# Fused attention and feed-forward kernel: fold of w3 and w_out moved into batch 0's attention, group 0's products behind it

## Chip, cores and metric

One core of a Trainium2 chip. The metric is the device time of one execution in microseconds. The kernel before takes 327.4 us (median of three runs, 326.2 to 327.7). An execution more than 1.5% above the fastest of its kernel counts as slow.

## The reference, cut to what matters

```python
# q, k, v: 8 batches x 8 heads x 576 x 64, f32
scores = q @ k.T / sqrt(64), masked to 0 <= i - j < 64      # causal window
attn   = softmax(scores) @ v                                 # -> x: 4608 x 512
a = x @ w1;  b = x @ w2                                      # 512 x 1024 each
out = ((a * b) @ w3) @ w_out                                 # 1024 x 1024, 1024 x 512
```

Nothing nonlinear lies between w3 and w_out, so the kernel forms their product once (the **fold**, 1024 x 512) and multiplies a*b by it.

## The kernel before: the parts concerned

PE does the matmuls; ACT, DVE and GpSimd (POOL in profiles) copy, mask and multiply; SP issues loads. PE writes into PSUM buffers, and a buffer can be used again when another engine has read it. PE is called warm when its granted clock is 1.0 (a matmul of 512 columns every 0.216 us in these traces) and cold at half of it (every 0.427 us).

Work goes in batches (attention, six steps each) and in groups of 512 tokens (eight blocks of a*b, four output blocks). The instructions of an engine stand in the order of the program, and one that waits holds up those behind it: in the change ACT stands idle for 5.21 us in front of a cast while copies that PE needs stand behind it. Line numbers in profiles are those of the kernel that was run; the same statement has other numbers in other versions.

```python
ps_s, ps_v, ps_t: one buffer each;  ps_f: bufs=3      # PSUM: scores, values, transposes, the rest

def scores(d):      # PE: 4 matmuls -> s_ps;  ACT: exp -> pt;  GpSimd: two masks a part
def values(d):      # PE: 8 matmuls -> o_ps;  ACT: ln, ln, exp;  DVE: two multiplies -> xT
def ffn_ab(g, fc):  # PE: 8 matmuls -> a_ps, b_ps (ps_f);  ACT: copy of a;  DVE: times b -> ab
def ffn_o(g, t):    # PE: 8 matmuls ab x wc -> ps_f;  DVE: copy;  store
def fold_t(fc):     # PE: 8 transposes of w3 -> ps_f;  DVE: copy
def fold_mm(fc):    # PE: 8 matmuls with w_out -> ps_f;  ACT: cast -> wc
...
load_qk(0, "k"); load_qk(0, "q")               # on the SP queue
...
pool_cp(gate, raws["k", 0][0:1, 0, 0:1])       # start gate: GpSimd waits for a first piece of k
for c in (0, 2, 3): load_v(0, c)               # all v and weight loads are on GpSimd's queue
for i in range(2): load_w12(i)
for c in (4, 5): load_v(0, c)
ones_of(1)                                     # memset for batch 1's v, on GpSimd
load_wo()
...  # batch 0: scores and values, with pieces of group 0's a*b between them (cut)
...  # then loads of w3, fold steps 0 to 2, batch 1's transposes, fold step 3
scores(6); fold_step(4); scores(7); values(6); fold_step(5); scores(8); values(7)
...  # and so on: one fold step, later one output block, beside each step of batch 1
```

From group 1 on, a schedule places a*b and output blocks between the attention steps; the change does not touch its principle.

## Time and profile before

| | before |
|---|---|
| last fold product on PE, started | 84.5 us |
| first a*b of group 1, started | 98.3 us |
| useful PE time lost until then | 45.9 us |
| the same, until 180 us | 53.6 us |
| time | 327.4 us |

The slices of the granted clock show that in this kernel PE is mostly warm after the opening. (The opening and later gaps hold dummy matmuls, `keep_busy`, whose results nobody reads; they are meant to keep the clock up.) Each digit is one of 40 equal slices, in tenths:

```profile
PEclk9765979998999789999999999999999999999796
```

### The profile page before, as it was taken

The page shows a single profiled execution, that of the slowest core. Times are in us where ns is not written, and L with a number is a line of the kernel's source. Part 1 is how long each engine was busy: PE and PEld are TensorE (multiplying, and loading weights), DVE is VectorE, ACT ScalarE, POOL GpSimd, SP SyncE. Part 2 cuts the span into 40 slices and gives each one's busy share as a digit, 9 for nine tenths or more (in the row PEclk, how much of TensorE's full clock was granted, in tenths as well). Part 3 has the DMA queues.
Part 4 walks back from the last instruction along what each step waited for, and adds up shares of the span by engine and source line. Part 5 has one row for each costly group of instructions (what it writes and reads, how often), then busy time and mean ns, then how long its engine had stood idle before and what let it go on. Part 6 is the DMA issues. An engine that isn't in the chain of part 4 may idle for free.

```text
span 327.4 us, 5810 instructions
## 1 busy us (share of the span) xinstructions
PE 285.9 (87%) x2151; PEld 177.9 (54%) x2151; DVE 195.6 (60%) x299; ACT 185.2 (57%) x308; POOL 178.6 (55%) x214
## 2 busy tenths in 40 slices
PE   4477599958899699999999999999999999996880
PEld 4465498535454455655555589555555555442330
DVE  5842545462378457977777776669767656545240
ACT  2246644656845367678778766487678766532200
POOL 8736493006891789679777856496785552200000
PEclk9765979998999789999999999999999999999796
DMA  7999969500049969496587664680293030030021
GB/s 214 314 341 250 198 106 180 59 0 0 3 82 253 306 157 89 161 246 42 119 297 65 94 214 144 70 134 3 22 162 21 2 123 7 2 130 2 4 98 41
DMA packets 52247, 38.91 MB, mean 119 GB/s; under 512 B 39360, under 2 KB 42432, under 8 KB 52208
## 3 DMA queue, kind: packets, MB, share of 16 engines
q0 software_dynamic: 41808, 9.96, 32.6%
q1 hardware_dynamic: 10400, 28.47, 24.5%
q8 instruction: 19, 0.31, 0.4%
q14 instruction: 20, 0.16, 0.2%
HBM read 38.80 MB, written 9.44 MB: 147 GB/s over the span
## 4 chain that ended last, share of the span: by engine, by line
PE 72%; DMA 11%; ACT 5%; DVE 4%; issue 3%; POOL 2%; SPq 0%; DVEq 0%; POOLq 0%; ACTq 0%
PE f_ps L392 36%; PE f_ps L405 18%; DMA w_sb<-in_moe_w_dram 8%; PE o_ps L306 6%; PE s_ps L271 4%; PE f_ps L451 4%; DMA stage<-in_k_dram 4%; PE tp L248 3%; ACT ln_s L316 1%; ACT r L318 1%; DVE xT L322 1%; POOL v L230 1%; DVE qT L257 1%; POOL k L215 1%; PE f_ps L443 1%
## 5 line engine op out<-in xcount | busy, mean ns | idle before, releaser
L392 PE MATMUL f_ps<-xT,w_sb 128*128 128x512 f16 (+3 forms) x768 | 139.9, 334 | 4.0 <-DVE xT L322 2.9
L392 PEld LDWEIGHTS <-w_sb 128*128 128x128 f16 x768 | 70.3, 100 | 51.3 <-issue 7.7
L285 POOL TENSOR_SCALAR_AFFINE_SELECT pt<-pt 128x512 f16<-128x512 f16 (+1 forms) x64 | 52.7, 823 | 82.4 <-ACT pt L276 82.4
L405 PE MATMUL f_ps<-wc_sb,ab 128*128 128x512 f16 x288 | 67.1, 379 | 0.1
L398 DVE TENSOR_TENSOR ab<-f_ps,a_sb 128x512 f16<-128x512 f32 (+1 forms) x74 | 49.9, 676 | 27.0 <-PE f_ps L392 25.1
L321 DVE TENSOR_TENSOR xT<-o_ps,r 64x384 f16<-64x384 f32 x48 | 26.4, 550 | 59.1 <-ACT r L318 59.1
L276 ACT ACTIVATE pt<-s_ps 128x1024 f16<-128x1024 f32 (+1 forms) x48 | 45.7, 952 | 27.5 <-PE s_ps L271 26.0
L397 ACT COPY a_sb<-f_ps 128x512 f32<-128x512 f32 (+1 forms) x74 | 42.0, 567 | 32.7 <-PE f_ps L392 32.1
L287 POOL TENSOR_SCALAR_AFFINE_SELECT pt<-pt 128x512 f16<-128x512 f16 (+1 forms) x64 | 52.7, 823 | 4.4
L315 ACT ACTIVATE ln_s<-o_ps 64x384 f32<-64x384 f32 x48 | 23.4, 487 | 36.8 <-PE o_ps L306 36.7
L405 PEld LDWEIGHTS <-ab 128*128 128x128 f16 x288 | 27.0, 98 | 27.6 <-issue 0.3
L230 POOL DMA_DIRECT2D v<-in_v_dram x40 | 34.1, 858 | 3.9 <-DMA v<-in_v_dram 2.1
L306 PE MATMUL o_ps<-pt,v 128*128 128x128 f16 (+1 forms) x384 | 29.0, 220 | 6.2 <-DVE xT L322 2.2
L306 PEld LDWEIGHTS <-v 128*128 128x128 f16 x384 | 24.8, 101 | 16.1 <-issue 2.7
L271 PE MATMUL s_ps<-qT,kT 128*128 128x256 f16 x192 | 28.7, 275 | 4.0 <-DVE qT L257 3.1
L407 DVE COPY t2k<-f_ps 128x512 f32<-128x512 f32 x36 | 24.9, 691 | 8.8 <-PE f_ps L405 8.0
L322 DVE TENSOR_TENSOR xT<-o_ps,r 64x384 f16<-64x384 f32 x48 | 26.9, 561 | 0.6
L271 PEld LDWEIGHTS <-kT 128*128 128x128 f16 x192 | 18.8, 103 | 15.0 <-issue 5.5
L318 ACT ACTIVATE r<-ln_s 128x384 f32<-128x384 f32 x48 | 25.1, 522 | 1.5
L316 ACT ACTIVATE ln_s<-o_ps 64x384 f32<-64x384 f32 x48 | 23.2, 482 | 0.6
L257 DVE COPY qT<-tp 64x768 f16<-64x768 f16 x18 | 17.3, 961 | 7.9 <-ACT qT L257 7.6
L252 DVE COPY kT<-tp 128x768 f16<-128x768 f16 x18 | 17.1, 950 | 3.9 <-PE tp L248 3.8
(52 smaller groups left out, 208.0 us busy)
## 6 DMA issues: line engine op xcount, KB each, us to landing
stage<-in_k_dram SPq DMA_DIRECT2D x32, 288.0 KB, 4.0
stage<-in_q_dram SPq DMA_DIRECT2D x32, 288.0 KB, 5.5
out_dram<-t2k SPq DMA_DIRECT2D x36, 256.0 KB, 2.0
v<-in_v_dram POOLq DMA_DIRECT2D x32, 128.0 KB, 4.0
w_sb<-in_moe_w_dram POOLq DMA_DIRECT2D x4, 512.0 KB, 24.1
ab<-in_moe_w_out_dram POOLq DMA_DIRECT2D x1, 1024.0 KB, 24.3
ab<-in_moe_w_dram POOLq DMA_DIRECT2D x4, 256.0 KB, 5.1
xT<-in_moe_w_dram POOLq DMA_DIRECT2D x4, 256.0 KB, 9.5
```

The lines of the kernel that those rows point to most:

```text
L230: nc.gpsimd.dma_start(out=vh[lo:P, c], in_=v[b, :, s0:s0 + P - lo, :].rearrange("h s d -> s h d"))
L271: nc.tensor.matmul(s_ps[:, jj, c0:c0 + 2 * n].rearrange("k (a n) -> k a n", a=2), kT[:, 2 * jp + jj, k0:k0 + P], qT[:, 2 * jp + jj, :, q0: ...
L276: nc.scalar.activation(pt[:, :, 0:w], s_ps[:, :, 0:w], AF.Exp, bias=-SHIFT, scale=scale)
L285: nc.gpsimd.affine_select(out=sl, in_=sl, pattern=pat, compare_op=ALU.is_ge, fill=0.0, base=off, channel_multiplier=-1)
L287: nc.gpsimd.affine_select(out=sl, in_=sl, pattern=[[-s, m] for s, m in pat], compare_op=ALU.is_ge, fill=0.0, base=63 - off, channel_multip ...
L306: nc.tensor.matmul(o_ps[:, jj, o0:o0 + n], v16[:, si * 2 + bi, j0 + jj, a * D:a * D + P], pt[:, jj, c0 + a * n:c0 + a * n + n], start=firs ...
L318: nc.scalar.activation(r, y, AF.Exp, scale=-1.0)
L322: nc.vector.tensor_tensor(xs[D:P], o_ps[D:P, :, 192:384], r[D:P], ALU.mult)
L392: nc.tensor.matmul(d[:, f * n + c0:f * n + c1], w[:, dc, (fc + f) * P:(fc + f + 1) * P], xT[:, dc, xc:xc + c1 - c0], start=first, stop=(dc ...
L397: act_cp(a_sb[:, 0:nf * n], a_ps[:, 0:nf * n])
L398: nc.vector.tensor_tensor(ab[:, fc:fc + nf, lo:hi], b_ps[:, 0:nf * n].rearrange("p (f n) -> p f n", f=nf), a_sb[:, 0:nf * n].rearrange("p ...
L405: nc.tensor.matmul(o_ps, ab[:, fc, t * P:t * P + P], wc_sb[:, fc, :], start=(fc == 0), stop=(fc == 7))
```

## The change

Intent: use the time in which PE waits for w1 and w2. w_out and w3 are loaded first, the fold goes between batch 0's steps; w1 and w2 come last, as all of group 0's a*b follows the fold; its output goes between batch 1's steps. Loads of batch 1's k and q, which ran beside the weights, are held back by a one-column memset into their buffer, which DVE does only after fold step 6; those of batch 2 by one on GpSimd.

The diff, cut to its core:

```diff
-    def load_qk(b, which):
+    def load_qk(b, which, gate=None):
         t = sb.tile([P, 2, TI * D], FP32, name="stage", bufs=4)
+        if gate is not None:
+            gate(t[:, 0, 0:1], 0.0)
...
     make_identity(nc, ident16)
+    load_wo()
+    load_w3(0)
+    load_w3(1)
...
-    pool_cp(gate, raws["k", 0][0:1, 0, 0:1])
     for c in (0, 2, 3):
         load_v(0, c)
-    for i in range(2):
-        load_w12(i)
+    load_w3(2)
     for c in (4, 5):
         load_v(0, c)
+    load_w3(3)
+    for half in range(2):
+        for i in range(2):
+            load_w12(i, half)
     ones_of(1)
-    load_wo()
...
+    for d in range(6):
+        if d < 5:
+            scores(d + 1)
+        if d == 3:
+            copy_v(0, 4)
+        if d < 5:
+            fold_step(d + 1)
+        values(d)
+    fold_step(6)
+    load_qk(1, "k", nc.vector.memset)
+    load_qk(1, "q")
+    fold_step(7)
...
+    for c in range(3):
+        cast_third(1, "k", c, act_cp if c != 1 else dve_cp)
+    for c in range(3):
+        cast_third(1, "q", c, act_cp if c != 1 else pool_cp)
+    for c in (0, 2, 3, 4, 5):
+        load_v(1, c)
+    for fc in range(8):
+        ffn_ab(0, fc)
+        if fc in (4, 5, 6):
+            transposes(1, "k", fc - 4)
...  # q transposes of batch 1
+    ffn_o(0, 0)
+    scores(6)
+    load_qk(2, "k", nc.gpsimd.memset)
...
+    for d in range(6, 12):
+        values(d)
+        if d < 10:
+            scores(d + 2)
+        if d in (7, 9):
+            ffn_o(0, (d - 3) // 2)
...
-        first = 3 if g == 1 else 0
+        first = 5 if g == 1 else 0
```

Batch 2's q transposes move to the fourth, fifth and sixth a*b block of group 1.

More of the change, by code (lines that the diff above doesn't have):

```diff
@@ L239, with transposes @@
     kTs = {}
-    def transposes(b, which, c, early=False):
+    def transposes(b, which, c, tp=None, late=True):
         if c == 0 and which == "k":
@@ L245, in transposes @@
         t16 = (k16s if which == "k" else q16s)[b]
-        tp = ps_f.tile([P, 6, P], FP16, name="f_ps") if early else ps_t.tile([P, 6, P], FP16, name="tp")
+        if tp is None:
+            tp = ps_t.tile([P, 6, P], FP16, name="tp")
         for i in range(6):
@@ L250, in transposes @@
         if which == "k":
-            cp = act_cp if early and c == 1 else dve_cp
+            cp = dve_cp if late or c != 1 else act_cp
             cp(kTs[b].rearrange("q j (p i) -> q j p i", i=TI)[:, :, :, 6 * c:6 * c + 6], src)
@@ L422, in w3_rows, with load_w12 @@
             xT[:, fc - 4, 2 * S:2 * S + DF].rearrange("p (a n) -> p a n", a=2)
-    def load_w12(i):
-        for half in range(2):
-            cols = slice(half * 512, half * 512 + 512)
-            nc.gpsimd.dma_start(out=(w1_sb, w2_sb)[i][:, :, cols],
-                                in_=(moe_w1, moe_w2)[i][:, cols].rearrange("(c p) n -> p c n", p=P))
+    def load_w12(i, half):
+        cols = slice(half * 512, half * 512 + 512)
+        nc.gpsimd.dma_start(out=(w1_sb, w2_sb)[i][:, :, cols],
+                            in_=(moe_w1, moe_w2)[i][:, cols].rearrange("(c p) n -> p c n", p=P))
     def load_wo():
@@ L433, in load_w3 @@
     def load_w3(n):
-        for fc in (2 * n, 2 * n + 1):
-            nc.gpsimd.dma_start(out=w3_rows(fc),
-                                in_=moe_w3[fc * P:fc * P + P].rearrange("p (a n) -> p a n", a=2))
+        fc = 2 * n
+        dst = w3a[:, 2 * fc:2 * fc + 4, :].rearrange("p (f a) n -> p f (a n)", f=2) if n < 2 else \
+            xT[:, fc - 4:fc - 2, 2 * S:2 * S + DF]
+        nc.gpsimd.dma_start(out=dst, in_=moe_w3[fc * P:fc * P + 2 * P].rearrange("(f p) n -> p f n", p=P))
     def fold_t(fc):
@@ L446, in fold_t, with fold_mm @@
         return w3T
-    def fold_mm(fc, w3T):
+    def fold_mm(fc, w3T, cp):
         o_ps = ps_f.tile([P, DM], FP32, name="f_ps")
@@ L451, in fold_mm @@
             nc.tensor.matmul(o_ps, w3T[:, ec, :], wo16[:, ec, :], start=(ec == 0), stop=(ec == 7))
-        act_cp(wc_sb[:, fc, :], o_ps)
+        cp(wc_sb[:, fc, :], o_ps)
     def check_sums():
@@ L487 @@
     ones_of(0)
-    gate = const.tile([1, 1], FP32)
-    pool_cp(gate, raws["k", 0][0:1, 0, 0:1])
     for c in (0, 2, 3):
         load_v(0, c)
-    for i in range(2):
-        load_w12(i)
+    load_w3(2)
     for c in (4, 5):
         load_v(0, c)
+    load_w3(3)
+    for half in range(2):
+        for i in range(2):
+            load_w12(i, half)
     ones_of(1)
-    load_wo()
-    keep_busy(45)
-    cast_third(0, "k", 0, dve_cp)
-    cast_third(0, "k", 1, act_cp)
-    cast_third(0, "k", 2, dve_cp)
@@ L502 @@
-    for c in range(3):
-        transposes(0, "k", c, early=True)
-    keep_busy(15)
-    cast_third(0, "q", 0, dve_cp)
-    cast_third(0, "q", 1, act_cp)
-    cast_third(0, "q", 2, dve_cp)
-    for c in range(3):
-        transposes(0, "q", c, early=True)
-    keep_busy(25)
-    w3Ts = {}
-    scores(0)
-    scores(1)
-    copy_v(0, 1)
-    values(0)
-    keep_busy(8)
-    scores(2)
-    values(1)
-    keep_busy(8)
-    scores(3)
-    ffn_ab(0, 0, 2, 0, 192)
-    values(2)
-    scores(4)
-    copy_v(0, 4)
@@ L525 @@
-    ffn_ab(0, 2, 2, 0, 192)
-    values(3)
-    scores(5)
-    load_w3(0)
-    load_w3(1)
-    ffn_ab(0, 0, 2, 192, 384)
-    values(4)
-    ffn_ab(0, 2, 2, 192, 384)
-    load_qk(1, "k")
-    load_qk(1, "q")
-    for fc in (4, 6):
-        ffn_ab(0, fc, 2, 0, 192)
-    values(5)
-    for fc in (4, 6):
-        ffn_ab(0, fc, 2, 192, 384)
-    ffn_ab(0, 0, 4, 384, 512)
-    for c in (0, 2, 3):
-        load_v(1, c)
-    load_w3(2)
-    load_w3(3)
-    for c in (4, 5):
-        load_v(1, c)
-    ffn_ab(0, 4, 4, 384, 512)
+    w3Ts = {}
@@ L550, in fold_step @@
     def fold_step(fc):
+        if fc == 0:
+            w3Ts[0] = fold_t(0)
         if fc + 1 < 8:
             w3Ts[fc + 1] = fold_t(fc + 1)
-        fold_mm(fc, w3Ts.pop(fc))
-    w3Ts[0] = fold_t(0)
-    for fc in range(3):
-        fold_step(fc)
-        cast_third(1, "k", fc, act_cp)
-    for c in range(3):
-        cast_third(1, "q", c, act_cp if c != 1 else dve_cp)
-        transposes(1, "k", c, early=True)
-    load_qk(2, "k")
-    load_qk(2, "q")
+        fold_mm(fc, w3Ts.pop(fc), act_cp if fc % 4 == 3 else dve_cp)
@@ new lines, in spare @@
+    def spare(pool, name):
+        t = pool.tile([P, 2, 512], FP32, name=name).bitcast(FP16)
+        return [t[:, i, 0:768].rearrange("p (i n) -> p i n", i=6) for i in range(2)]
+    keep_busy(60)
+    tps = spare(ps_s, "s_ps") + spare(ps_v, "o_ps")
+    for c in range(3):
+        cast_third(0, "k", c, act_cp if c == 1 else dve_cp)
+    for c in range(3):
+        transposes(0, "k", c, tps[c], late=False)
+    keep_busy(15)
+    for c in range(3):
+        cast_third(0, "q", c, act_cp if c == 1 else dve_cp)
@@ new lines @@
+    transposes(0, "q", 0, tps[3])
+    transposes(0, "q", 1)
+    tps = spare(ps_s, "s_ps")
+    transposes(0, "q", 2, tps[0])
+    keep_busy(10)
+    w3Ts[0] = fold_t(0)
+    scores(0)
+    w3Ts[1] = fold_t(1)
+    copy_v(0, 1)
+    fold_mm(0, w3Ts.pop(0), dve_cp)
+    for d in range(6):
[8 more added lines that the diff above has]
+    load_qk(1, "k", nc.vector.memset)
@@ L564 @@
+    load_qk(1, "q")
+    fold_step(7)
     for n in range(3):
         keep_sums(n)
-    fold_step(3)
     for c in range(3):
-        transposes(1, "q", c, early=True)
+        cast_third(1, "k", c, act_cp if c != 1 else dve_cp)
+    for c in range(3):
+        cast_third(1, "q", c, act_cp if c != 1 else pool_cp)
[5 more added lines that the diff above has]
+            transposes(1, "k", fc - 4)
+    tps = spare(ps_v, "o_ps")
@@ L569 @@
+    for c in range(3):
+        transposes(1, "q", c, tps[c] if c < 2 else None)
     copy_v(1, 1)
+    ffn_o(0, 0)
     scores(6)
-    fold_step(4)
+    load_qk(2, "k", nc.gpsimd.memset)
+    load_qk(2, "q")
+    store()
+    ffn_o(0, 1)
     scores(7)
-    values(6)
     copy_v(1, 4)
-    fold_step(5)
-    scores(8)
-    values(7)
-    cast_qk(2, "k", 0, pool_cp)
-    fold_step(6)
-    scores(9)
-    values(8)
-    cast_qk(2, "k", 1, pool_cp)
-    fold_step(7)
-    scores(10)
-    values(9)
-    ffn_o(0, 0)
@@ L587 @@
-    cast_qk(2, "q", 0, pool_cp)
-    scores(11)
-    transposes(2, "k", 0)
-    values(10)
-    load_v(2, 0)
-    store()
+    store()
+    for d in range(6, 12):
[4 more added lines that the diff above has]
+            ffn_o(0, (d - 3) // 2)
+            store()
+        if d in (8, 9):
+            cast_qk(2, "k", d - 8, pool_cp)
+            load_v(2, (d - 8) * 2)
+    cast_qk(2, "q", 0, pool_cp)
     cast_qk(2, "q", 1, pool_cp)
-    ffn_o(0, 1)
@@ L595 @@
-    load_v(2, 2)
+    load_qk(3, "k")
+    load_qk(3, "q")
     load_v(2, 3)
-    transposes(2, "k", 1)
-    store()
-    ffn_o(0, 2)
-    values(11)
-    transposes(2, "k", 2)
-    store()
-    load_qk(3, "k")
     load_v(2, 4)
     load_v(2, 5)
-    ffn_o(0, 3)
-    store()
-    load_qk(3, "q")
     for n in range(3, 6):
@@ L623 @@
             slots.append((w, lo + (hi - lo) * share + (LAG + 1) * (i >= first)))
-    todo = {0: [lambda: transposes(2, "q", 0), lambda: cast_qk(3, "k", 0, pool_cp), lambda: copy_v(2, 1)],
-            1: [lambda: transposes(2, "q", 1), lambda: cast_qk(3, "k", 1, pool_cp)],
-            2: [lambda: transposes(2, "q", 2), lambda: copy_v(2, 4)]}
+    todo = {0: [lambda: transposes(2, "k", 0)], 1: [lambda: transposes(2, "k", 1)],
+            2: [lambda: transposes(2, "k", 2), lambda: copy_v(2, 1), lambda: cast_qk(3, "k", 0, pool_cp)],
+            3: [lambda: transposes(2, "q", 0), lambda: cast_qk(3, "k", 1, pool_cp)],
+            4: [lambda: transposes(2, "q", 1), lambda: copy_v(2, 4)], 5: [lambda: transposes(2, "q", 2)]}
     u = 24
```

## The prediction

> **What bounds the kernel now.** I read the page's slices first, to see where TensorE is not full.
>
> ```profile
> span 327.4 us, 5810 instructions
> PE   4477599958899699999999999999999999996880
> DMA  7999969500049969496587664680293030030021
> ```
>
> A slice is 8.2 us. From slice 14 (about 115 us) PE is full until the tail. A gain or a loss must come from the first 113 us; afterwards the kernel only works off what is left. The chain of waits agrees: from 113 us on it is almost all PE, before that it steps through DMA, ACT and DVE. DMA is full for the first 42 us, and empty from about 60 to 90 us.
>
> The table of stretches gives the same by size:
>
> ```profile
> core 0: us, PE busy (x) PEld busy (x) DVE busy (x) ACT busy (x) POOL busy (x), PEclk, DMA share, GB/s
> 0.00:20.00 20.00, 11.17 (x114) 10.83 (x115) 13.68 (x13) 5.96 (x7) 14.32 (x19) 0.78 1.05 279
> 60.00:80.00 20.00, 15.43 (x125) 9.14 (x123) 8.38 (x13) 12.01 (x20) 4.14 (x8) 0.91 0.01 1
> 120.00:140.00 20.00, 20.00 (x144) 11.56 (x143) 14.92 (x24) 15.30 (x26) 16.09 (x18) 1.00 0.63 114
> ```
>
> Busy PE time in the opening is partly dummy matmuls and half-clock ones, so I count useful work instead. From the chain at full clock: eight 512-wide matmuls 1.73 us, eight 128-wide 0.45, four 256-wide 0.44. So: one a*b block 1.73 (group 0: 8, 13.8 us); one output block 1.73 (group 0: 4, 6.9); one fold step 0.45+1.73 = 2.18 (8: 17.4); one attention step 0.89; six transposes 6 x 0.056 = 0.34.
>
> The first a*b of group 1 starts at 98.32 us. By then PE has done 13.8 + 6.9 + 17.4 + 12 x 0.89 + 15 x 0.34 = 53.9 us of useful work: 44.4 us are lost. Another 5 us go by 113.5, mostly here:
>
> ```profile
> 99.33 8.60 DMA stage<-in_k_dram
> 108.13 2.25 POOL k L215 x2
> ```
>
> Pool waits for batch 3's k, and the transposes queued in front of the scores wait for Pool. The change has to lower 44.4 + 5.
>
> Then I read how GpSimd issues its loads, because the change makes it issue all ten MB of weights before batch 0's masks:
>
> ```profile
> 4.33 2.78 POOL L230 DMA_DIRECT2D v<-in_v_dram  x3
> 7.07 3.04 POOL L427 DMA_DIRECT2D w_sb<-in_moe_w_dram  x4
> 10.07 0.73 POOL L230 DMA_DIRECT2D v<-in_v_dram  x1
> 12.20 0.88 POOL L230 DMA_DIRECT2D v<-in_v_dram  x1 [1.40 <-DMA v<-in_v_dram]
> 18.17 0.87 POOL L431 DMA_DIRECT2D ab<-in_moe_w_out_dram  x1 [2.42 <-DMA v<-in_v_dram]
> ```
>
> Eight loads go out without a wait. The ninth waits until the first has landed (4.33 + 7.6 us), the tenth for the second. The loads at 43 to 53 us repeat it: the 21st, 22nd and 23rd wait for the 13th, 14th and 15th. So load n waits for load n-8, and Pool stands still meanwhile.
>
> Last, one attention step in the timeline, since both orders are paced by it:
>
> ```profile
> 80.52 0.50 PE L306 MATMUL o_ps<-pt,v 128*128 128x128 f16 x8 [0.92 <-DVE xT L322]
> 81.06 0.49 ACT L315 ACTIVATE ln_s<-o_ps 64x384 f32<-64x384 f32 x1 [0.34 <-PE o_ps L306]
> 82.08 0.52 ACT L318 ACTIVATE r<-ln_s 128x384 f32<-128x384 f32 x1
> 83.20 0.56 DVE L322 TENSOR_TENSOR xT<-o_ps,r 64x384 f16<-64x384 f32 x1
> 83.90 0.61 PE L306 MATMUL o_ps<-pt,v 128*128 128x128 f16 x8
> ```
>
> The one o_ps buffer comes free 3.4 us after its values began. Batch 1's six values start at 76.5, 80.5, 83.9, 87.8, 91.3 and 95.5: 3.4 to 4.2 us apart, although a fold step and an attention step need only 3.07 us of PE. I use 3.5 us.
>
> **What the Trainium skill says.** "DMA: Bandwidth & Descriptors", Specifications, gives an HBM limit of about 358 GB/s per core. The trace agrees: 14.5 MB (k and q of three batches 7.1, v 1.2, w1, w2 and w_out 6.3, all read as f32) from 2.2 us to w_out's landing at 42.5 are 360 GB/s. The same page, Issuing engines are not separate DMA queues, says loads of all engines share the same DMA engines and interleave; here w1's first half, issued at 7.07, took 21 us while k and q of batches 1 and 2 went through. "TensorE: Matmul & The Clock Gate", What's actually happening, has the clock fall to half after an idle window of about 3.4 us. The trace fits: after PE's wait near 70 us eight 512-wide matmuls took 3.46 us at 72.87, and 1.90 once warm.
>
> **Part 1, loads.** The change removes the start gate, puts w_out and half of w3 ahead of v and w1/w2 last, and holds back k and q of batch 1 by a DVE memset, of batch 2 by a Pool memset. Landings, worked out from the rates above: q of batch 0 about 12 us as now. Beside it w_out gets perhaps a third, then 410 GB/s (5.1 us for its 2.1 MB from 37.4 to 42.5 in the trace): w_out at 15, the first two w3 quarters at 17.6 and 20.2 (2.6 us each), v's three pieces 21.3, 22.4, 23.5 (1.1 us apart at 52 to 55 us in the trace), all of w3 at 30, w1/w2 at about 41. That is 5 us later than now for w1/w2, but nothing needs them before.
>
> By the rule of eight the 14th load goes out when the 6th, v's third piece, has landed: 23.6 us, 0.8 for it, then the memset of ones for batch 1 (2.7 us in the trace) to 27.1. Only then come the masks of scores 0: 0.63+0.64+0.42+0.42 with gaps, 2.2 us. Values 0 starts at 29.3, against 23.9 now, though its scores can be ready at 18 (q's casts no longer run beside that memset, where one took 3.9 us). Two fold products (4.4 us) fill part of the gap, and PE goes idle about 5 us.
>
> **Part 2, folds in batch 0.** Values 5 starts 5 x 3.5 later, 46.8. Its DVE work ends 3.24 later, 50.0; then DVE has the last w3 copy and a cast (0.69 each), so the memset that releases k of batch 1 comes at 51.5. PE ends the fold at 52.5. The fold is 34 us earlier than now (86.4), w1/w2 have been there for 11 us, and DMA has stood idle for 10.
>
> **Part 3, a*b of group 0.** Here I see the main cost. k and q of batch 1 (2.36 MB) need 6.6 us at 360 GB/s and 2.2 us to begin, so q lands at 60.5. Their casts stand ahead of group 0's copies of a in ACT's order. PE can fill three f_ps buffers (2.6 us, to 55.1) and then waits: q at 60.5, two ACT casts of 0.84 to 62.2, the first copy of a 0.59 to 62.8. 7.7 us of idle PE, and about 1.7 for the half clock after it. The rest, 13.8 - 2.6 = 11.2, with three k transposes 1.0, ends at 76.7; q transposes 77.7. Scores 6 come 3.0 us after (as from 69.0 to 71.98 now): 80.7.
>
> **Part 4, output between batch 1's steps.** Values 6: scores 0.5, exp 0.8, masks 2.2, hand-overs 0.3: 84.5. Values 11 at 84.5 + 17.5 = 102.0. The first a*b of group 1 follows 2.8 later, as now (95.5 to 98.3): 104.8. PE has only four output blocks to put into these 20 us, where now it has five folds as well; the steps stay paced by o_ps.
>
> **Part 5, entry into the steady state.** Five a*b blocks of group 1 run ahead of the first tick instead of three, and k of batch 3 comes early, so the 8.6 us DMA wait goes. But q's last transposes come right before scores 12: 2.2 us for their copies, then exp and masks before values 12. I put 4 us lost against 5.
>
> **Sum.** At 104.8 the useful work is 53.9 - 3 x 0.34 = 52.9, lost 51.9 against 44.4: +7.5. Entry -1. Net +6.5, 327.4 + 6.5 = 334.
>
> **Rivals.** (a) The intended gain. PE has useful matmuls in the weights' wait; if values 0 started at 24 and casts did not block, 5 + 8 + 2 us vanish and the time is about 319. For it: weights now stop PE until 33.6. Against it: the rule of eight and the order of ACT's work follow from code and trace. (b) A wash. If the steps of batch 0 run faster than 3.5 us (Pool needs 2.2, PE 3.07), or HBM gives k and q sooner, each recovers 2 to 3 us: 327 to 330. (c) Worse: steps at 4 us, as the slower of batch 1's are, plus a half clock in each idle, 5 us more: 339.
>
> **Range and chances.** The two stalls (5 and 8 us) are firm in kind, their sizes to 2 or 3 us; clock and steps add as much. A change so carefully arranged may avoid something I overlook, so I keep some weight on a gain. 324 to 342. The 2% limits are 320.8 and 333.9: faster 0.08, within 0.42, slower 0.50.
>
> **What would show it.** Pool's w1/w2 issues spread to about 24 us, each after a landing, and the first mask at 27; values 0 near 29; DMA empty from about 41 to 52; ACT idle until q of batch 1 lands near 60 with PE idle beside it for 8 us; group 1's first a*b near 105; after about 120 the same picture as now, shifted. I am wrong if Pool reaches the masks by 23, if q of batch 1 lands before the fold ends, or if group 1 starts before 98.

## More of the kernel before

"Lost" is the time of day minus the useful matmuls recorded up to it, each at the full-clock rate of 0.216 us for 512 columns; dummy matmuls do not count. A trace can miss a few matmul records, so a level can be a few us too high; differences are safer.

## The result, and the profile after

347.96 us (four runs, 346.97 to 349.33) against 327.4 us for the kernel before in the same session (median of three; the record's 327.51 has the slow fourth in it): ratio 1.064, 95% interval 1.059 to 1.070. Ratios here and below are the mean time of one kernel's fast runs over that of the other's of the same rounds, so not quite the ratio of the medians quoted. The direction was right; the size, +20.6 us, was three times the +6.5 predicted and outside the range of 324 to 342.

The page of the kernel after, in slices of 8.6 us:

```profile
span 345.9 us, 5523 instructions
PE   6486955497674977999999999999999999998790
PEclk9589999599766696999999999999999999999896
DMA  7999706840467950768768767574049011020021
```

PE is full only from slice 16 (138 us), where before it was slice 14 of 8.2 us (115 us). DMA has a hole in slice 5 (43 to 52 us), as predicted. New are the clock digits 5 in slice 7 (60.5 to 69 us) and 6 and 7 in slices 10 to 13 and 15 (86 to 121 and 130 to 138 us), where the kernel before has 7 to 9.

Two stalls were predicted, and both came. GpSimd's loads, from the timeline of after:

```profile
9.79 0.77 POOL L232 DMA_DIRECT2D v<-in_v_dram  x1
17.23 1.27 POOL L232 DMA_DIRECT2D v<-in_v_dram  x1 [6.67 <-DMA ab<-in_moe_w_out_dram]
19.70 0.70 POOL L439 DMA_DIRECT2D xT<-in_moe_w_dram  x1 [1.20 <-DMA ab<-in_moe_w_dram]
22.19 0.78 POOL L429 DMA_DIRECT2D w_sb<-in_moe_w_dram  x1 [1.80 <-DMA ab<-in_moe_w_dram]
23.66 2.34 POOL L429 DMA_DIRECT2D w_sb<-in_moe_w_dram  x3 [0.69 <-DMA v<-in_v_dram]
25.98 2.68 POOL L491 MEMSET v<- 128x3072 f16 x1
28.60 0.66 POOL L288 TENSOR_SCALAR_AFFINE_SELECT pt<-pt 128x512 f16<-128x512 f16 x1
```

The ninth load waits for the first (w_out), the tenth and eleventh for the second and third, and the first mask comes after the memset: 28.6 (predicted 27.1), values 0 at 30.0 (predicted 29.3). Then the stall ahead of group 0's a*b:

```profile
52.69 0.06 DVE L206 MEMSET stage<- 128x1 f32 x1
53.94 2.75 PE L395 MATMUL f_ps<-xT,w_sb 128*128 128x512 f16 x12
59.93 1.56 ACT L224 CAST k<-stage 128x768 f16<-128x768 f32 x2 [5.21 <-DMA stage<-in_k_dram]
63.03 1.56 ACT L224 CAST q<-stage 128x768 f16<-128x768 f32 x2 [1.53 <-DMA stage<-in_q_dram]
64.50 1.06 ACT L400 COPY a_sb<-f_ps 128x512 f32<-128x512 f32 x2
65.13 8.81 PE L395 MATMUL f_ps<-xT,w_sb 128*128 128x512 f16 x28 [8.44 <-ACT a_sb L400]
```

The memset releases k at 52.7 (predicted 51.5); PE fills three banks and stands idle for 8.44 us (predicted 7.7) until ACT has cast q and then copied a. The last line also shows the part I had put at 1.7 us: 28 matmuls took 8.81 us, 6.05 at the full-clock rate. And the clock stays low, as these lines from batch 1's steps show:

```profile
92.65 0.80 PE L309 MATMUL o_ps<-pt,v 128*128 128x128 f16 x8 [2.44 <-DVE xT L325]
94.10 3.62 PE L408 MATMUL f_ps<-wc_sb,ab 128*128 128x512 f16 x8
97.51 0.73 PE L309 MATMUL o_ps<-pt,v 128*128 128x128 f16 x8
```

An output block took 3.62 us; warm, the same row has 1.89. The step that it is in lasts 4.9 us instead of 3.5.

| point | predicted | measured | added since the line above |
|---|---|---|---|
| values 0 starts | 29.3 | 30.0 | +0.7 |
| fold ends on PE | 52.5 | 54.1 | +0.9 |
| q of batch 1 there | 60.5 | 63.0 | +0.9 |
| PE resumes a*b | 62.8 | 65.1 | -0.2 |
| k transposes and a*b of group 0 done | 76.7 | 80.0 | +1.0 |
| scores 6 starts | 80.7 | 85.6 | +1.6 |
| values 6 starts | 84.5 | 88.5 | -0.9 |
| values 11 starts | 102.0 | 108.9 | +2.9 |
| first a*b of group 1 runs on | 104.8 | 112.7 | +1.0 |
| lost from there to 180 us | about 4 | 11.5 | |

(Two of the first a*b block's eight matmuls ran at 109.7.) The lost time at 180 us is 72.3 us against 53.6 before: 18.7, close to the difference of the two profiled spans, 345.9 - 327.4 = 18.5.

### The profile page after: what moved, and what is told of

It is laid out like the page before. It is cut to its first block, busy times and chain, and to the rows that moved or that the text cites. A ratio compares the mean times of both kernels' runs of the same rounds, so it can differ in the third digit from the quotient of the medians.

```text
span 345.9 us, 5523 instructions
## 1 busy us (share of the span) xinstructions
PE 288.4 (83%) x2007; PEld 168.4 (49%) x2007; DVE 198.1 (57%) x305; ACT 180.2 (52%) x298; POOL 178.0 (51%) x211
## 4 chain that ended last, share of the span: by engine, by line
PE 59%; DVE 2%; ACT 2%; issue 1%; POOL 1%; DVEq 0%; POOLq 0%; ACTq 0%
PE f_ps L395 32%; PE f_ps L408 16%; PE o_ps L309 4%; PE s_ps L274 4%; PE tp L251 3%; DVE qT L260 1%; ACT qT L260 0%; DVE xT L325 0%; ACT r L321 0%; POOL pt L290 0%; POOL pt L288 0%; ACT ln_s L319 0%; DVE okv L464 0%; DVE chk L461 0%; ACT pt L279 0%
## 5 line engine op out<-in xcount | busy, mean ns | idle before, releaser
L395 PE MATMUL f_ps<-xT,w_sb 128*128 128x512 f16 (+1 forms) x640 | 142.3, 373 | 10.4 <-ACT a_sb L400 8.4
L288 POOL TENSOR_SCALAR_AFFINE_SELECT pt<-pt 128x512 f16<-128x512 f16 (+1 forms) x64 | 52.7, 823 | 82.5 <-ACT pt L279 82.4
L395 PEld LDWEIGHTS <-w_sb 128*128 128x128 f16 x640 | 62.3, 101 | 67.0 <-issue 21.5
L401 DVE TENSOR_TENSOR ab<-f_ps,a_sb 128x512 f16<-128x512 f32 x72 | 49.7, 691 | 35.9 <-PE f_ps L395 26.7
L408 PE MATMUL f_ps<-wc_sb,ab 128*128 128x512 f16 x288 | 69.7, 390 | 0.1
L400 ACT COPY a_sb<-f_ps 128x512 f32<-128x512 f32 x72 | 41.6, 579 | 44.9 <-PE f_ps L395 44.5
L408 PEld LDWEIGHTS <-ab 128*128 128x128 f16 x288 | 27.7, 100 | 29.5 <-issue 3.1
L260 DVE COPY qT<-tp 64x768 f16<-64x768 f16 x20 | 19.2, 960 | 7.8 <-ACT qT L260 7.6
L255 DVE COPY kT<-tp 128x768 f16<-128x768 f16 x21 | 19.9, 950 | 2.1 <-PE tp L251 2.0
```

Of the source, the lines that this page charges most:

```text
L288: nc.gpsimd.affine_select(out=sl, in_=sl, pattern=pat, compare_op=ALU.is_ge, fill=0.0, base=off, channel_multiplier=-1)
L395: nc.tensor.matmul(d[:, f * n + c0:f * n + c1], w[:, dc, (fc + f) * P:(fc + f + 1) * P], xT[:, dc, xc:xc + c1 - c0], start=first, stop=(dc ...
L400: act_cp(a_sb[:, 0:nf * n], a_ps[:, 0:nf * n])
L401: nc.vector.tensor_tensor(ab[:, fc:fc + nf, lo:hi], b_ps[:, 0:nf * n].rearrange("p (f n) -> p f n", f=nf), a_sb[:, 0:nf * n].rearrange("p ...
L408: nc.tensor.matmul(o_ps, ab[:, fc, t * P:t * P + P], wc_sb[:, fc, :], start=(fc == 0), stop=(fc == 7))
```

## The experiments

All kernels gave the right result. They ran in three sessions of four, on three chips; the kernel before ran beside them at 327.1, 327.4 and 328.0 us. Three rounds each, four runs of each experiment. Theory A is the prediction's: PE starves because batch 1's k and q arrive late in front of ACT's copies, because GpSimd reaches the masks late, and because the steps hold too little matmul work. Rival B: the pace of the steps sets the end, whatever comes before.

**The hold on k and q removed.**

```diff
-    load_qk(1, "k", nc.vector.memset)
+    load_qk(1, "k")
```

> The change with the DVE memset that holds back batch 1's k and q taken away, nothing else. Theory A (the 8 us of idle PE before group 0's a*b come from q of batch 1 landing at 63 while ACT has its casts in front of the copies of a): the idle goes, but 2.36 MB now run ahead of the weights, so by 6.6 us of transfer w_out and the v pieces land later, values 0 start near 36 instead of 30.0, and the fold ends near 60 instead of 54. Together with the idle (8.4) and the half clock behind it saved: 344 to 347, against 348 for the change. Rival B (the time lost here is given back or taken again by the later attention steps, whatever comes before): within 1 us of 348. Rival C (the order of the loads does not matter because DMA has room): 338.

345.6 us (ratio 1.055, interval 1.047 to 1.062). As expected: values 0 goes back from 30.0 to 36.2 and the fold ends at 62.9 instead of 54.1, and a*b runs without the long idle (1.5 us are left of it). What the hold gained at the start was lost again behind it: the two times differ by 2.3 us, with overlapping intervals.

**The hold released earlier.**

```diff
         values(d)
+        if d == 2:
+            load_qk(1, "k", nc.vector.memset)
+            load_qk(1, "q")
     fold_step(6)
-    load_qk(1, "k", nc.vector.memset)
-    load_qk(1, "q")
```

> The same memset and the same loads of batch 1's k and q, but issued after values 2 of batch 0 instead of after fold 6; by then (41 us) the weights have landed. Theory A: k lands near 47, q near 51, before the fold ends at 54, so PE goes from the last fold straight into a*b: 8.4 us of idle and about 1.5 us of half clock vanish, 338. Rival B: unchanged within 1 us, because the chain of attention steps of batch 1 sets the end.

338.7 us (1.035, 1.031 to 1.039). As expected; 9.3 us less than the change (measured in another session). Rival B falls.

**Loads as in the change, casts behind a*b.**

```diff
-    casts of k and q of batch 1, loads of v
     for fc in range(8):
         ffn_ab(0, fc)
+        if fc == 3: casts of k
+        if fc == 6: casts of q, loads of v
```

> Loads and memset as in the change; only the casts of batch 1's k stand behind the fourth a*b block of group 0 and those of q behind the seventh, in ACT's, DVE's and GpSimd's order. Theory A says that it is the order on ACT and not the landing that stops PE: q still lands at 63, but a*b begins at 54 and runs on, the idle of 8.4 us goes to under 1 us, 338 to 340. If it is the landing itself that binds (rival D, the transposes of k and q), the idle moves behind a*b and the time stays above 344. v of batch 1 is issued some 5 us later here, which should not bind.

336.3 us (1.027, 1.022 to 1.031), a little better than expected: 11.6 us less than the change. In the timeline of this version k is released no earlier than in the change (54.4 us), yet PE runs 40 matmuls, five whole a*b blocks, without a break:

```profile
54.43 0.06 DVE L206 MEMSET stage<- 128x1 f32 x1
55.68 8.80 PE L395 MATMUL f_ps<-xT,w_sb 128*128 128x512 f16 x40
62.40 1.57 ACT L224 CAST k<-stage 128x768 f16<-128x768 f32 x2
```

So it is the order of the casts that stopped PE, not the landing of k. The run moves those on DVE and GpSimd too; in the change ACT is the engine that ends last: DVE is through with its cast of k at 60.5, ACT with q at 64.6.

**Masks ahead of the w1 and w2 loads.**

```diff
-    for half in range(2): ... load_w12(i, half)
-    ones_of(1)
...
             scores(d + 1)
+        if d == 0:
+            for half in range(2): ... load_w12(i, half)
+            ones_of(1)
```

> The four loads of w1 and w2 and the memset of ones for batch 1 go behind scores 1's masks in GpSimd's order, nothing else. Theory A: GpSimd reaches the first mask as soon as the exp of scores 0 is done (23.6 us instead of 28.6), values 0 starts near 26 instead of 30.0, and all that follows is 4 us earlier: 344. w1 and w2 land a few us later and still before they are needed. Rival E (v's landing or the fold sets the start of values 0): within 1 us of 348.

348.8 us (1.066, 1.061 to 1.070): no gain, the expectation of 344 was wrong. The first mask did come at 24.0 us. But GpSimd still has to do the 5.7 us of issuing and memset, and now does them ahead of scores 2's masks:

```profile
28.11 0.50 PE L309 MATMUL o_ps<-pt,v 128*128 128x128 f16 x8
29.18 3.00 POOL L429 DMA_DIRECT2D w_sb<-in_moe_w_dram  x4
32.14 2.71 POOL L491 MEMSET v<- 128x3072 f16 x1
37.14 0.61 PE L309 MATMUL o_ps<-pt,v 128*128 128x128 f16 x8 [2.54 <-POOL pt L290]
```

Values 0 (28.1) is 1.9 us earlier than in the change, values 2 (37.1) starts only 0.4 us before the change's third (37.6), and the clock drops in the gap. Moving GpSimd's work within the stretch gains nothing; taking it out does, as a later run shows.

**Dummy matmuls in batch 1's steps**, on top of the late casts.

```diff
         if d in (7, 9):
             ffn_o(0, (d - 3) // 2)
             store()
+        else:
+            keep_busy(40 if d == 11 else 18)
```

> On top of the late casts (336.3): dummy matmuls after the steps of batch 1 that have no output block (18 each, about 1 us at full clock, 40 after the last)[...]. Theory C (a good part of the loss here is the half clock of a starved PE): the first two a*b blocks of group 1, 2.9 and 3.2 us there, take 2.1, and one step of 4.0 us becomes 3.5: 333 to 334. Rival: the steps are paced by the one o_ps buffer at 3.4 to 3.5 us whatever the clock, and the gain is under 1 us.

332.9 us (1.020, 1.013 to 1.026), 3.4 us less than without the dummies; the two come from different sessions and their intervals overlap, but none of the four runs of either reaches into the other's. As expected: the first a*b blocks of group 1 follow each other at 2.1 to 2.4 us. So part of the loss is the half clock and not only the waits. With the late casts the steps were already mostly warm, so this run does not measure what the half clock cost in the change itself; the early release does (see why the prediction was wrong).

**Batch 2's q transposes earlier**, on top of the late casts.

```diff
-    3: [q, third 0 ...], 4: [q, third 1 ...], 5: [q, third 2]      # all through the one ps_t bank
+    0: [k 0, q 0 through s_ps], 1: [k 1, q 1 through o_ps], ..., 3: [q 2 ...]
```

> On top of the late casts (336.3): batch 2's q transposes go ahead, the first two through the score and value banks beside k's, the third behind the fourth a*b block, so that their copies are done before scores 12. Theory: the entry into the steady state loses time because the three q transposes share one bank and each waits about 2 us for ACT's and then DVE's copy of the one before (125 to 131 us in the change); this takes away some 5 us: 331 to 332. Rival: exp and masks of scores 12 and 13 set the entry; then under 2 us.

334.7 us (1.023, 1.014 to 1.031). The expectation of -5 us was wrong; the gain is about 1.6 us and the two ratios come from different sessions, with intervals that overlap. The waits between the transposes are gone, the masks of scores 12 and 13 remain.

**Both.**

> Both of the two before together. If their gains lie in different stretches they add: 328 to 330. If the half clock is only a consequence of the waits at the entry, little beyond the larger of the two.

330.4 us (1.008, 1.002 to 1.015), just above the 328 to 330 expected: a gain from the transposes is there again (2.6 us against the dummies alone, in the same session), and the two add.

**A*b of group 0 between batch 1's steps.** Early release, v of batch 1 issued between batch 0's steps, casts of k and q around fold step 6, and:

```diff
+    for fc in range(3):
+        ffn_ab(0, fc); transposes(1, "k", fc)
+    transposes(1, "q", ...)              # through s_ps, o_ps, tp
+    ffn_ab(0, 3); scores(6); ...; ffn_ab(0, 4); scores(7); ...; ffn_ab(0, 5)
+    for d in range(6, 12):
+        values(d)
+        if d < 10: scores(d + 2)
+        if d < 8:  ffn_ab(0, d)
+        else:      ffn_o(0, d - 8); store()
```

> Other placement of group 0's a*b, to test the claim that the change loses because batch 1's steps have too little matmul work between them: early release of batch 1's k and q (after values 2), v of batch 1 issued between batch 0's steps, four a*b blocks with the transposes, the other four between batch 1's scores and values, the output blocks in its last steps, q of batch 2 early as in the entry variant. If starved steps are the cause: fold ends at 54, group 1 begins near 86 instead of 112.7, and the time is 311 to 318, faster than the kernel before. If the steps merely get longer by the blocks put in (a bound on ACT, DVE or GpSimd), the time stays at 327 or above.

320.5 us (0.981, 0.976 to 0.986): faster than the kernel before, but 2.5 us above the expected 311 to 318. Group 1 begins at 88.8 (expected 86). A step of this version, from its timeline:

```profile
79.61 0.61 PE L309 MATMUL o_ps<-pt,v 128*128 128x128 f16 x8 [0.71 <-DVE xT L325]
80.49 1.89 PE L408 MATMUL f_ps<-wc_sb,ab 128*128 128x512 f16 x8
83.10 0.61 PE L309 MATMUL o_ps<-pt,v 128*128 128x128 f16 x8 [0.71 <-DVE xT L325]
```

PE still waits for o_ps, 0.71 us instead of the 2.44 seen in the change, and the step keeps its 3.5 us with a block in it at full clock.

**The same without the interleaving**: all eight blocks ahead of scores 6.

```diff
-    ffn_ab(0, 3) ... ffn_ab(0, 7) spread over scores 6 to values 7
+    for fc in range(3, 8):
+        ffn_ab(0, fc)
```

> The interleaved version (320.5) with all eight a*b blocks of group 0 ahead of scores 6, everything else the same, loads included. It measures what blocks between batch 1's steps are worth by themselves. If starved steps are the cause: each step still takes 3.4 to 3.5 us, the four moved blocks add 4 x 1.73 = 6.9 us ahead of them: 327 to 328. If the gain of that version came from the early loads: within 1 us of 320.5.

330.8 us (1.009, 1.002 to 1.016), 10.3 us more, where the moved blocks were expected to cost 6.9. Not all of it is theirs. In the profiled pair, 12.1 us apart, the fold already ends 3.6 us later here (58.4 against 54.7), in a stretch in which the two programs are the same: from 30.6 to 37.5 us PE was granted 0.51 of its clock here and 1.00 there. About 8.5 us are left for the blocks and for the clock behind them, which falls again. The stretch from 54 to 90 us, first of the interleaved version, then of this one (columns as in the prediction; PEclk is the third from the right):

```profile
54.00:90.00 36.00, 30.07 (x211) 16.19 (x210) 20.50 (x33) 22.33 (x38) 19.25 (x25) 1.00 0.36 95
```

```profile
54.00:90.00 36.00, 27.84 (x165) 14.69 (x164) 17.95 (x28) 19.36 (x30) 9.75 (x15) 0.83 0.29 75
```

The two busy shares look alike; the clock does not. The loads are the same in both, so it is where the blocks stand, and not the early loads, that separates the two.

**The start gate put back into the change.**

```diff
     make_identity(nc, ident16)
+    pool_cp(gate, raws["k", 0][0:1, 0, 0:1])
     load_wo()
```

> The change with the kernel before's start gate put back: GpSimd issues no weight load until the first quarter of batch 0's k is there. In the change k is cast at 12.1 us and q at 16.7, where the kernel before had 7.7 and 12.2, because w_out runs beside them. Theory: this delay is hidden, since values 0 waits for GpSimd's first mask (28.6), which waits for the chain of loads; k and q come 4 us earlier again, the weights 1 to 3 us later, and the time is 348 to 350. Rival F (the later k and q are a part of the 20 us lost): 344.

348.4 us (1.064, 1.055 to 1.073), as expected. In the change k and q of batch 0 are cast at 12.1 and 16.7 us, 4 us later than before, which I had not foreseen. With the gate k is back at 8.2 and q at 13.9, and values 0 still starts at 30.8. The delay is hidden behind the masks.

**Batch 1's ones on DVE**, on top of the interleaved version.

```diff
     ones_of(0)
+    ones_of(1)                       # now nc.vector.memset, while DVE is idle
...
-    ones_of(1)
```

> On top of the interleaved version (320.5): batch 1's memset of ones goes from GpSimd, where it stands between the loads and the first mask, to DVE at the start, where DVE is idle. Theory: the first mask comes 2.7 us sooner, at 26, values 0 near 27.5 to 28 instead of 30.0 (two fold products stand ahead of it on PE), and all behind it shifts: 318 to 319. Rival: as with the masks put first, the gain is eaten later in the same stretch: within 1 us of 320.5.

317.7 us (0.968, 0.962 to 0.975), a little better than the 318 to 319 expected, and the fastest version: 3.2% faster than the kernel before. The first mask comes at 26.05, values 0 at 28.6.

**v first in the opening**, several moves at once on top of that: start gate, v's pieces ahead of w_out and w3, w1 and w2 behind scores 1's masks, scores 0 ahead of the first w3 transposes, batch 1's k released after values 3.

> On top of the interleaved version (320.5), the opening rearranged so that nothing of batch 0's attention waits for weights: start gate, v's three first pieces ahead of w_out and w3, w1 and w2 issued behind scores 1's masks, ones on DVE, scores 0 ahead of the first w3 transposes, batch 1's k released after values 3. Theory (the opening is bound by the order on GpSimd's queue, not by the sum of transfers): values 0 near 25 instead of 30.0, fold end near 49, 314 to 317. Rival: the weights' landing moves back by as much as the masks move forward, within 1 us of 320.

320.7 us (0.979, 0.972 to 0.986), against an expected 314 to 317: no gain over the interleaved version, and 3.0 us more than with ones on DVE alone. Scores 0 is ready at 18.9, but the fold product ahead of values 0 now waits for the later w3, and runs on a cold PE:

```profile
22.02 1.89 PE L446 MATMUL f_ps<-ident,ab 128*128 128x128 f16 x16 [2.66 <-DMA ab<-in_moe_w_dram]
23.84 3.45 PE L454 MATMUL f_ps<-ab,t2k 128*128 128x512 f16 x8
```

Values 0 starts at 29.6 (28.6 with ones on DVE alone), though the first mask comes at 20.3. So in this bundle the order on GpSimd is no longer what holds it: what v gains w3 loses. Which of the moves costs the time was not tested.

## Why the prediction was wrong

**Right.** The rule that load n waits for load n-8, and the mask behind the memset. The sizes there agree in part by luck: the 14th issue came at 25.25 us instead of 23.6 (the 23.66 in the lines above is the 12th), which makes the first mask 1.5 us late, but values 0 starts behind two of its four masks, after 1.4 us, where the prediction counted all four, 2.2. The stall ahead of group 0's a*b: 8.4 us instead of 7.7, and its cause, the casts in front of the copies of a, is shown by the late casts, which take 11.6 us off with the loads of k and q unchanged. The hole in DMA. The picture after the entry: between 180 and 300 us the change loses less than 1 us more.

**Wrong in three terms, of size.** First, "about 1.7 for the half clock after it" in part 3, and no half clock at all in parts 4 and 5. Durations of rows that have a warm twin: 28 matmuls 8.81 instead of 6.05, output blocks 3.62 and 2.79 instead of 1.89, the remaining six matmuls of group 1's first block 2.72 instead of 1.30, two more whole a*b blocks of group 1 3.08 and 3.05 instead of 1.89. That is 2.8 + 1.7 + 0.9 + 1.4 + 1.2 + 1.2 = 9.2 us of excess duration, against 1.7 booked. Not all of it can be added to the end, since a step paced by o_ps hides some, and the last three belong to the entry below. For the steps of batch 1 two traces measure it. The early release has the same 72 matmuls in them as the change and the same waits for o_ps (2.44 us twice, 2.88 before the last). These are its five intervals between values 6 and values 11, and then the change's (columns as above):

```profile
80.60:98.60 18.00, 8.18 (x72) 4.91 (x72) 7.38 (x14) 11.70 (x20) 14.42 (x18) 1.00 0.72 199
88.47:108.88 20.41, 12.01 (x73) 6.83 (x72) 7.38 (x14) 11.71 (x20) 15.21 (x19) 0.73 0.63 178
```

At full clock they take 18.0 us, in the change 20.4; I had put 17.5. So 2.4 of the 2.9 us that these steps add are the half clock. I had seen that they have little PE work ("only four output blocks to put into these 20 us") and took 3.5 us a step, the lower end of what I had read in the kernel before, whose own five intervals take 19.0. Little PE work alone does not bring the clock down, though: in the early release it stays at 1.00. What decides between the two is not shown. I had rival (c), "steps at 4 us ... plus a half clock in each idle", at 339, and even that covers little more than half of the 20.6. The trace before could have warned me. I took it as agreeing with an idle window of 3.4 us, but the wait near 70 us that I read for this lasted 2.95:

```profile
71.98 0.49 PE L271 MATMUL s_ps<-qT,kT 128*128 128x256 f16 x4 [2.95 <-DVE qT L257]
72.87 3.46 PE L451 MATMUL f_ps<-ab,t2k 128*128 128x512 f16 x8
```

Second, the q transposes of batch 1, 1.0 us in part 3. They took 3.0 (80.0 to 83.0), because the second goes into the other half of the one o_ps buffer and waits for the copies of the first:

```profile
82.35 0.49 PE L251 MATMUL o_ps<-ident,q 128*128 128x128 f16 x6 [1.89 <-DVE qT L260]
```

Third, part 5, "I put 4 us lost against 5". The entry lost 11.5 us in the change (72.3 - 60.8); in the kernel before it was 7.7 (53.6 - 45.9). So instead of giving back 1 us it took 3.8. By stretches of the change: 2.7 with the first, cold a*b blocks up to 118.8; 3.3 around the waits of q's transposes through one bank, booked at 2.2 (idle 0.80, 0.16 and 1.89 us, before 125.90, 128.28 and scores 12 at 130.67); 4.5 from there to values 13 at 139.3, where exp, masks and the half clock come together; 1.0 later. Removing the waits of the transposes gave 1.6 to 2.6 us. How the 4.5 divide is not settled.

The miss in the profiled spans is 18.5 - 6.5 = 12.0. The terms give 12.7: 4.8 at the entry (3.8 + 1.0), and 7.9 up to group 1 (112.7 - 104.8), which by the table is 2.3 already there when PE resumes a*b, 1.0 more than booked for the half clock in it, 1.6 for q's transposes, -0.9 for the way to values 6, 2.9 for the steps and 1.0 for the start of group 1.

**A term that was right and misread.** Values 0 at 30 instead of 24 is there, but it is not a 5 us cost that comes off by moving GpSimd's work later (masks first: 348.8). Part of it comes off where work leaves GpSimd altogether (ones on DVE, on top of the interleaved version: 2.8 us).

**Where the intended gain went.** The change does fill the opening: at 54 us it has lost 29.9 us of PE, the kernel before at 55.5 us 34.7. Then it spends 8.4 us in front of ACT's casts, and takes from batch 1's steps the fold work that had filled them. Between those two points and group 1 the kernel before loses 11 us and the change 31. With a*b put where the fold was, and the casts out of the way, the early fold is worth having: 317.7 us.

## What to carry to other kernels

When work is moved to fill an early wait, ask what it filled where it came from: steps that a single buffer paces keep their length, so a block put between them is nearly free and a block taken out gives nothing back, and may cost the clock besides. Look along each in-order engine for an instruction that waits on a late load in front of one that the critical engine needs: moving six casts took 11.6 us off here, the earlier release of the loads 9.3. And before taking a step's duration from the old trace, allow for a colder engine in the new place: the same steps ran at full clock in one version here and at 0.73 of it in another.

## What the Trainium skill lacked or had wrong

- "TensorE: Matmul & The Clock Gate", What's actually happening, says that the array goes to half clock after an idle window of about 3.4 us. In batch 1's steps of the changed kernel no single idle of PE exceeded 2.9 us (2.44 before 92.65 and 101.12, 2.88 before 108.88), yet the granted clock was 0.73 there, and blocks ran at half clock (3.62 us instead of 1.89). The same waits passed at a clock of 1.00 in the early release. How much work in a window keeps the clock up is what one needs here; the page's account of a second failure mode, with short idles between groups of matmuls, does not give it either.
- No page has the limit of eight loads from GpSimd, and none needs it: it is in the program. The stored traces number the semaphores. In the change the first eight loads signal 104 to 111, and the ninth, which is to signal 104 again, first waits for it (17.23 us for w_out, 6.67 us of standing still); in the kernel before it is the same with 105 to 112. Whether the chip has a limit of its own these runs do not tell.
- "DMA: Bandwidth & Descriptors", Specifications, gives about 358 GB/s of HBM for a core, without a condition. Between 2.2 and 42.5 us the kernel before moved 360, but w_out alone, 2.1 MB in 5.1 us, ran at 410. The page is not wrong: its section on measured bandwidth gives 425 for one core alone and keeps about 358 each for two cores that stream at once. The table taken by itself misleads, and the 360 of the prediction is no limit that was reached.
